# Layer one of a linear-attention and gMLP kernel: the last two token blocks of the transposed expansion as seven block products

## The chip, the cores and the metric

The kernel runs on one core of a Trainium2 chip. The metric is the device time of one execution in microseconds (us), the median of several runs. The engines have short names here, as in the profile: PE (TensorE, matrix products), PEld (its weight loads), DVE (VectorE), ACT (ScalarE), POOL (GpSimd) and SP (SyncE, which issues most DMAs). Each engine works through its own list of instructions in order and waits on semaphores for the others.

## The reference

Two layers, each of a linear attention (A) and a gated MLP with a mixing over tokens (B), on 2048 tokens of 512 features, all in fp32:

```python
def _A_ref(x, wqkv, wo):            # S=2048, D=512, 32 heads of 16
    q, k, v = split(x @ wqkv)
    phi = lambda t: where(t > 0, t + 1, exp(t)) + 1e-6
    pq, pk = phi(q), phi(k)
    kv, z = sum_s pk v, sum_s pk
    return ((pq kv) / (pq z + 1e-6)) @ wo

def _B_ref(x, w_in, w_sp, b_sp, w_out):      # w_in: 512 x 1792, w_sp: 2048 x 2048
    z = gelu(x @ w_in)                       # z1: first 896 columns, z2: last 896
    g = w_sp @ layernorm(z2) + b_sp
    return (z1 * g) @ w_out

x = x + A(ln(x));  x = x + B(ln(x));  x = x + A(ln(x));  x = x + B(ln(x))
```

## The kernel before

Every fp32 operand is split into a high and a low fp32r part (`high` on ACT, L132; `low` on DVE, L135), and a product is three matmuls (`mm3`, L146 to L148). The order on every engine is written out by hand: a scheduler does not move anything, so a line that is called earlier in Python stands earlier in the list of each engine that it uses. Tiles come from slot pools (22 `pages` of 128x512, 6 `quads`, 4 `bigs`, 8 PSUM `banks`), first freed, first used.

Per layer there are three stages.

* `P1`, the attention's first half. For each of 16 token blocks of 128 (step `s`): layer norm (`ln_a`, `ln_b`), transposition through a DMA (`Turn`), splitting (`T_high`, `T_low`), projections `K` and `Q` of 12 matmuls each with their `phi`, and a Gram product `Gmm`. In layer one this is `first`, which also splits the weights `wo` and `win2` (the list `side`) from step 5 on; in layer two it is `second`, which spreads those pieces one per step and interleaves units of `Inner` with them. `ln_b` stores the normalised block for the transposition; `x_high`/`x_low` split the Gram operand.
* `P2`, steps `s` = 1 to 18. For token block `s-1` the attention's end (`c`, `c2` adds the residual, `c_stats`, `c3` normalises and sends the block through a DMA transposition), for block `s-2` the splitting of the transposed block (`d_high` on ACT behind a DVE transposition at L327, `d_low`), for block `s-3` the token-major half of the expansion (`e`, 24 matmuls of 448 columns, then `e2` gelu on ACT, `e3` statistics, `e4` normalisation on ACT of the previous block with scales that POOL makes at L265 to L270). The transposed half, `z1`, is made per chunk `n` of 512 tokens and feature group `f` of 128: `f()` takes 12 matmuls, a gelu and a store.
* `P4`, the mixing over tokens by nested block products, and then a loop over 16 token blocks for the output product.

Layer two (`seven`) does not make `z1` of the chunks 2 and 3 by `f()`. It sees the two chunks, the feature groups (`g`, `g+3`) and the two halves of the contraction as a 2x2x2 block product and takes seven products (`P1` to `P7` in the class `P2`, `product` at L967 to L969, 6 matmuls each) for each of three `g`; the seventh feature group is made by `last_f`. This needs sums of the token blocks (`block_sums`, five DVE operations at L924 to L934 per block; `block_parts` splits them) and sums of blocks of `win1`. The latter are made once by the class `Make` during layer one's last token loop, split, stored to DRAM in `kept`, and read back by `fetch_sum` through POOL's DMA queue (L949). Five of the seven products are in `tail`, after the loop over `s`; the steps `P1(g)` and `P2(g)` are in `side`.

Two other side works matter. `Sums.tick` makes sums of `w_sp` for the mixing in layer one: at the steps in `TOKEN_TICKS` (5, 6, 8, 9, 11, 12, 14, 17) three POOL additions (L1178). `Inner` makes and stores split sums for a nested product; one unit is a DVE addition, an ACT `high` and a DVE `low`. In layer one `P2` makes eight units of `N2`:

```python
elif s == 12:
    own.begin(2)
elif s == 13 or 15 <= s:
    own.unit()
```

Of the kernel before, what the change touches and what calls it, by code (L numbers as in the profile page):

```python
# [15 lines left out]
P = 128  # L16
# [3 lines left out]
NT = S // P  # L20
NCHK = S // 512
NF = FH // P
# [62 lines left out]
def mixer_kernel(ctx: ExitStack, tc: tile.TileContext, x_in, wqkv, wo_d, win1_d, win2_d, wsp_d, bsp_d, wout_d,  # L85
                 ident_d, mask_d, out_d):
    nc = tc.nc
# [7 lines left out]
    pages = Slots(main, "pg", 22)  # L95
    quads = Slots(main, "qd", 6)
# [37 lines left out]
    def low(l, src, h):  # L134
        nc.vector.tensor_sub(l, src, h.bitcast(F32))  # L135
# [196 lines left out]
    class P1:  # L332
# [236 lines left out]

        def first(self, side):  # L570
            ND = NT - DEFER
            self.wv = quads.get([P, 4, 512])
            for s in range(1, NT + 2):
                self.loadx(s + 3)
                self.turn.load(s + 1)
                turned = 2 <= s < NT and s not in self.turn.by_pe
                if turned:
                    self.T_high(s)
                if s == 1:
                    if not self.kb:  # L580
                        self.K(0)
                    self.K(1)
                elif 2 < s <= NT:
                    self.K(s - 1)
                self.ln_a(s + 2)
                if turned:
                    self.T_low(s)
                if s <= NT:
                    self.K_phi(s - 1)
                if s <= ND:  # L590
                    self.Q(s - 1)
                if s == NT + 1:
                    self.late()
                if s <= NT:
                    self.xsplit(s - 1)
                    self.K_split(s - 1)
                if s + 1 < NT and s + 1 in self.turn.by_pe:
                    self.T(s + 1)
                self.ln_b(s + 2)
                if s <= ND:  # L600
                    self.Q_phi(s - 1)
                if s >= 2:
                    self.Gmm(s - 2)
                if s == NT + 1:
                    self.late_phi()
                if s <= 4:
                    c = s - 1
                    nc.sync.dma_start(self.wv[:, c, :], wqkv[c * P:(c + 1) * P, 1024:1536])
                else:
                    for _ in range(min(len(side), 1 if s < 6 else 2)):  # L610
                        side.popleft().piece()
                if s >= 4:
                    for w in list(side)[:1 if s < 5 else 2]:
                        w.fetch()

        def second(self, side):
            ND = NT - DEFER
# [126 lines left out]
    class P2:  # L744
        def __init__(self, p1):
            self.L = L = p1.L
            self.p1 = p1
            self.win1, self.win2 = w_in1(), p1.win2
            self.qturn, self.xturn = Turn(f"qt{L}", range(3), True), Turn(f"yt{L}", range(4))
            self.qp, self.qT, self.x, self.ms, self.xB, self.z, self.zms = {}, {}, {}, {}, {}, {}, {}  # L750
            self.fq = deque()
            self.fnext = []
            self.seven = self.L == 1
            self.held = deque()
            self.S, self.T, self.Tp, self.X = {}, {}, {}, {}

# [91 lines left out]
        def d_low(self, i):  # L848
            b, home, h, l = self.dpart
            low(l, b, h)  # L850
            n, k = divmod(i, 4)
            if self.seven and n == 3:
# [5 lines left out]
            if k == 3 and not (self.seven and n >= 2):  # L858
                self.fnext = [(n, f) for f in range(NF)]

        def e(self, i):
# [28 lines left out]
        def f(self):  # L890
            if not self.fq:
                return False
            n, f = self.fq.popleft()
            h, l = self.xT[n]
            w = self.win1
            b = banks.get(PAGE)
            for c in range(4):
                mm3(b, (w.h[:, f, c, :], w.l[:, f, c, :]), (h[:, c, :], l[:, c, :]), c == 0, c == 3)
            if f == NF - 1 and not (self.seven and n >= 2):
# [153 lines left out]

        def run(self, sums):
            w1 = self.win1
            own = inner["N1" if self.seven else "N2"]
            for s in range(1, NT + 3):
                self.loadx(s + 1)
                self.qturn.load(s + 1)
# [26 lines left out]
                else:  # L1086
# [19 lines left out]
                    if s <= NT + 1:  # L1106
                        if not sooner:
                            self.d_high(s - 2)
                        if not self.seven and 14 <= s < 18:
                            own.unit()  # L1110
                        self.d_low(s - 2)
                if s >= 15:
                    self.block_sums()
# [11 lines left out]
                    self.e3(s - 3)  # L1125
                self.f()
                self.f()
                if self.seven:
                    self.side(s)
                    if s == 5:  # L1130
                        own.begin(2)
                    elif 6 <= s:
                        own.staged()
                elif s == 12:
                    own.begin(2)
                elif s == 13 or 15 <= s:
                    own.unit()
# [4 lines left out]
                if not self.seven:  # L1142
                    sums.tick(s, TOKEN_TICKS)
                if s >= NT + 1 and not self.seven:
                    self.p4.fetch(s - NT - 1)
            self.e4(NT - 1)
            self.win2.free()

# [179 lines left out]
    class P4:  # L1328
# [394 lines left out]

        def run(self, nxt):
            p2 = self.p2
            if p2.seven:
                p2.tail(self)
            else:
# [4 lines left out]
                p2.win1.free()  # L1733
                self.prepare(1, 1)
                self.fetch(3)
                self.prepare(None, 2)
# [75 lines left out]
            make = Make()  # L1812
            for i in range(NT):
                self.loadx(i + 2)
                self.gates(2)
# [80 lines left out]
```

## Time and profile before

| | us |
|---|---|
| median of 3 runs | 1364.96 |
| lowest, highest | 1364.62, 1366.05 |
| the profiled execution's own time | 1364.2 |
| its span, first to last instruction | 1362.2 |
| PE busy | 1355.5 |
| DVE busy | 1007.3 |
| ACT busy | 628.5 |
| POOL busy | 465.9 |

The granted clock of PE is 1.000 over the whole span. A line of the timeline reads: start in us from the span's start, duration, engine, line of the kernel, operation, tiles, shapes, count, and in brackets the idle time before it with what ended it. A row of a window reads: the window, its length, then busy time and count for PE, PEld, DVE, ACT and POOL, the clock, the share of the DMA engines and GB/s. The matmuls are pipelined, so a PE that is busy is not yet one that starts matmuls as fast as it can; the count per window tells that.

Layer one's `P1` runs to about 125 us of the span, its `P2` from about 150 to 328 us, its `P4` to about 700 us; layer two's `P2` ends at 1005 us.

### The profile page before, as it was taken

What the parts mean: (1) busy time and instruction counts of PE and PEld (TensorE: products, weight loads), DVE (VectorE), ACT (ScalarE), POOL (GpSimd) and SP (SyncE); (2) the same over time, 40 slices, a digit from 0 to 9 for tenths busy, and PEclk for the clock granted to TensorE, in tenths of its full rate; (3) what the DMA queues carried; (4) which work ended last, traced back from release to release, by engine and by line L of the source; (5) the groups of instructions that cost most, each with busy time, mean ns of one, the idle gap of its engine ahead of it and who ended that gap; (6) DMA issues with size and microseconds to landing.
All of it is one profiled execution on the core that took longest, in us unless ns stands there. A gap on an engine that the chain in (4) does not pass through costs nothing.

```text
span 1362.2 us, 18282 instructions
## 1 busy us (share of the span) xinstructions
PE 1355.5 (100%) x6105; PEld 1135.3 (83%) x6105; DVE 1007.3 (74%) x1541; ACT 628.5 (46%) x1004; POOL 465.9 (34%) x539
## 2 busy tenths in 40 slices
PE   9999999999999999999999999999999999999998
PEld 7888888888888888888888888888888888888887
DVE  7775888765756789978778758877767798878642
ACT  6775543444433443443466655534465534533310
POOL 3333475433233137427421133533230011312240
PEclk9999999999999999999999999999999999999999
DMA  5541377877778988797976523666568798568552
GB/s 178 172 132 63 116 247 255 262 248 272 258 250 282 310 266 284 266 367 246 329 241 201 189 94 116 209 203 205 188 204 282 220 339 321 196 200 316 215 182 89
DMA packets 182622, 306.95 MB, mean 225 GB/s; under 512 B 15488, under 2 KB 67584, under 8 KB 178432
## 3 DMA queue, kind: packets, MB, share of 16 engines
q1 hardware_dynamic: 174320, 265.81, 59.2%
q0 software_dynamic: 6336, 36.70, 7.4%
q10 hardware_dynamic: 1872, 3.28, 0.7%
q8 instruction: 48, 0.79, 0.2%
q14 instruction: 46, 0.38, 0.1%
HBM read 208.47 MB, written 97.26 MB: 224 GB/s over the span
## 4 chain that ended last, share of the span: by engine, by line
PE 97%; DVE 2%; ACT 1%; issue 0%; POOL 0%; DVEq 0%; ACTq 0%; POOLq 0%
PE bank L148 19%; PE bank L146 19%; PE bank L147 19%; PE bank L1585 9%; PE bank L1584 9%; PE bank L1586 9%; PE bank L1517 4%; PE bank L1518 4%; PE bank L1515 4%; PE bank L969 1%; PE bank L968 1%; PE bank L967 1%; PE bank L708 1%; PE bank L288 0%; DVE pg L135 0%
## 5 line engine op out<-in xcount | busy, mean ns | idle before, releaser
L1584 PE MATMUL bank<-qd,pg 128*128 128x512 f32 x544 | 211.6, 389 | 0.0
L1585 PE MATMUL bank<-qd,pg 128*128 128x512 f32 x544 | 211.6, 389 | 0.0
L1586 PE MATMUL bank<-qd,pg 128*128 128x512 f32 x544 | 211.6, 389 | 0.0
L1431 DVE TENSOR_TENSOR qd<-qd,qd 128x1024 fp32r<-128x1024 f32 x104 | 143.9, 1383 | 69.9 <-ACT qd L1422 69.6
L1422 ACT ACTIVATE qd<-qd 128x1024 fp32r<-128x1024 f32 x104 | 110.0, 1058 | 125.6 <-DVE qd L1431 49.4
L132 ACT ACTIVATE pg<-pg 128x512 fp32r<-128x512 f32 (+1 forms) x154 | 94.8, 620 | 134.3 <-DVE pg L327 46.3
L148 PE MATMUL bank<-qd,pg 128*128 128x512 f32 x380 | 148.5, 391 | 0.2 <-DVE pg L135 0.2
L1178 POOL TENSOR_TENSOR pg<-pg,pg 128x512 f32<-128x512 f32 x64 | 95.6, 1493 | 136.4 <-DMA pg<-in_wsp_dram 88.2
L265 POOL TENSOR_SCALAR rs<-mv 128x1 f32<-128x1 f32 x95 | 46.7, 492 | 261.4 <-DVE mv L263 252.4
L276 ACT ACTIVATE pg<-pg,nb,rs 128x512 f32<-128x512 f32 x63 | 51.3, 814 | 171.3 <-POOL nb L270 159.7
L1606 POOL TENSOR_TENSOR bg<-bg,pg 128x512 f32<-128x512 f32 x56 | 90.9, 1634 | 112.4 <-DMA pg<-z 99.9
L135 DVE TENSOR_TENSOR pg<-pg,pg 128x512 fp32r<-128x512 f32 (+1 forms) x151 | 112.9, 748 | 14.7 <-ACT pg L132 6.4
L1584 PEld LDWEIGHTS bank<-qd,pg 128*128 128x128 f32 x544 | 102.1, 188 | 21.4
L1586 PEld LDWEIGHTS bank<-qd,pg 128*128 128x128 f32 x544 | 102.1, 188 | 21.1
L1585 PEld LDWEIGHTS bank<-qd,pg 128*128 128x128 f32 x544 | 102.1, 188 | 21.1
L146 PE MATMUL bank<-qd,pg 128*128 128x512 f32 x284 | 110.8, 390 | 0.0
L147 PE MATMUL bank<-qd,pg 128*128 128x512 f32 x284 | 110.6, 389 | 0.0
L327 DVE STREAM_TRANSPOSE pg<-pg 128x512 f32<-128x512 f32 x79 | 85.6, 1084 | 14.1 <-DMA z<-pg 4.6
L146 PE MATMUL bank<-bg,qd 128*128 128x448 f32 x256 | 94.0, 367 | 0.0
L147 PE MATMUL bank<-bg,qd 128*128 128x448 f32 x256 | 93.6, 366 | 0.0
L148 PE MATMUL bank<-bg,qd 128*128 128x448 f32 x256 | 93.4, 365 | 0.0
L1517 PE MATMUL bank<-qd,pg 128*128 128x512 f32 x224 | 87.3, 390 | 0.1
(214 smaller groups left out, 3163.3 us busy)
## 6 DMA issues: line engine op xcount, KB each, us to landing
qd<-s SPq DMA_DIRECT2D x64, 512.0 KB, 4.1
qd<-n POOLq DMA_DIRECT2D x32, 1024.0 KB, 8.5
pg<-in_wsp_dram SPq DMA_DIRECT2D x103, 256.0 KB, 4.5
qd<-in_wsp_dram SPq DMA_DIRECT2D x40, 512.0 KB, 4.4
n<-pg SPq DMA_DIRECT2D x70, 256.0 KB, 4.4
s<-pg SPq DMA_DIRECT2D x64, 256.0 KB, 4.1
pg<-z SPq DMA_DIRECT2D x56, 256.0 KB, 4.2
x<-pg SPq DMA_DIRECT2D x48, 256.0 KB, 3.0
```

The costliest lines, as they stand in the source:

```text
L132: nc.scalar.activation(h, src, AF.Copy)
L135: nc.vector.tensor_sub(l, src, h.bitcast(F32))
L146: nc.tensor.matmul(out, ah, bh, start=start, stop=False)
L147: nc.tensor.matmul(out, ah, bl, start=False, stop=False)
L148: nc.tensor.matmul(out, al, bh, start=False, stop=stop)
L1178: nc.gpsimd.tensor_tensor(t, a, b, op=OP.add)
L1422: nc.scalar.activation(wh, r, AF.Copy)
L1431: nc.vector.tensor_sub(wl, r, wh.bitcast(F32))
L1517: m(out[i], h[:, o, f], w[:, o, 1], start=False, stop=False, skip_group_check=True)
L1584: m(out, h[:, o], w[:, 0, j, :], start=start, stop=False, skip_group_check=True)
L1585: m(out, h[:, o], w[:, 1, j, :], start=False, stop=False, skip_group_check=True)
L1586: m(out, l[:, o], w[:, 0, j, :], start=False, stop=stop, skip_group_check=True)
```

## The change

1. In layer one, too, `z1` of the chunks 2 and 3 is made by seven products: the conditions on `seven` go, `side` and `tail` run in both layers. Instead of 14 groups of 12 matmuls there are 21 products of 6 and two groups of 12, 150 instead of 168. The twelve gelu results of these products are stored through ACT's DMA queue instead of SP's.
2. `Make` moves from layer one's last token loop to layer one's `P2`, each step at the end of an iteration `s`: fetches at 7, 10, 12, additions one step later, the two splits two and three steps later, stores behind them. For the third group that is: four additions at `s` = 13, a split each at 14 and 15.
3. The eight units of `N2` move from layer one's `P2` to `first`, steps 2 to 9, in the staged form of layer two, with two quads as their store.
4. `first` takes the order of `second`: `x_high` and `x_low` early, one piece of `side` per step from step 2, between `K_high` and `K_low`; `ln_b` goes behind `Q_phi`; `wv` is loaded at step 15.
5. `d_high` is called `sooner`, before `c3`, from step 14 on in layer one too. The first two fetches for `P4` move from the steps 17 and 18 into `tail`.

```diff
-MAKE_AT = 0, 2, 4
+MAKE_AT = 7, 10, 12
+ROW_UNITS = range(2, 10)
...
         def first(self, side):
             ND = NT - DEFER
-            self.wv = quads.get([P, 4, 512])
+            own = inner["N2"]
+            spare = quads.get([P, 2, 2, 512]), quads.get([P, 2, 2, 512])
+            own.home = Views(pages, *spare)
             for s in range(1, NT + 2):
                 self.loadx(s + 3)
                 self.turn.load(s + 1)
+                if s <= NT:
+                    self.x_high(s - 1)
...
-                self.ln_a(s + 2)
+                if s <= NT:
+                    self.x_low(s - 1)
                 if turned:
                     self.T_low(s)
+                self.ln_a(s + 2)
...
                 if s <= NT:
-                    self.xsplit(s - 1)
-                    self.K_split(s - 1)
+                    lows = deque()
+                    if s > 1 and side:
+                        for _ in range(min(len(side), 1 if s < 10 else 2)):
+                            side.popleft().piece(lows=lows)
+                    self.K_high(s - 1)
+                    own.staged(s in ROW_UNITS)
+                    for l, src, h, r in lows:
+                        low(l, src, h)
+                        pages.put(r)
+                    self.K_low(s - 1)
                 if s + 1 < NT and s + 1 in self.turn.by_pe:
                     self.T(s + 1)
-                self.ln_b(s + 2)
                 if s <= ND:
                     self.Q_phi(s - 1)
+                self.ln_b(s + 2)
...
     class P2:
         def run(self, sums):
             w1 = self.win1
-            own = inner["N1" if self.seven else "N2"]
+            own = inner["N1"]
+            make = Make() if self.L == 0 else None
...
-                    sooner = self.seven and s >= 14
+                    sooner = s >= 14
...
-                if self.seven:
-                    self.side(s)
-                    if s == 5:
-                        own.begin(2)
-                    elif 6 <= s:
-                        own.staged()
-                elif s == 12:
+                self.side(s)
+                if self.L == 0:
+                    make.step(s)
+                elif s == 5:
                     own.begin(2)
-                elif s == 13 or 15 <= s:
-                    own.unit()
+                elif 6 <= s:
+                    own.staged()
...
     class P4:
         def run(self, nxt):
             p2 = self.p2
-            if p2.seven:
-                p2.tail(self)
-            else:
-                self.prepare(0, 0)
-                self.fetch(2)
-                while p2.f():
-                    pass
-                ...
+            p2.tail(self)
...
-                    make.step(i)
                     self.join(i, nxt)
```

`Make.step`, which is not changed, is what is called at the new place:

```python
def split(self, g):
    r = self.raw[g].pop()
    h = pages.get(PAGE, F32R)
    split(h, r.bitcast(F32R), r)      # high on ACT, then low on DVE
    self.part[g] = h.bitcast(F32), r, h
```

More of the change, by code (lines that the diff above doesn't have):

```diff
@@ L605, in first @@
                     self.late_phi()
-                if s <= 4:
-                    c = s - 1
-                    nc.sync.dma_start(self.wv[:, c, :], wqkv[c * P:(c + 1) * P, 1024:1536])
-                else:
[L610 to L614, printed above, removed]
+                for w in list(side)[:1 if s < 9 else 2]:
+                    w.fetch()
+                if s == 1:
+                    own.begin(2, 1)
+                if s == NT - 1:
+                    own.home.close()
+                    own.home = pages
+                    quads.put(*spare)
+                    self.wv = quads.get([P, 4, 512])
+                    for c in range(4):
+                        nc.sync.dma_start(self.wv[:, c, :], wqkv[c * P:(c + 1) * P, 1024:1536])
         def second(self, side):
@@ L851, in d_low @@
             n, k = divmod(i, 4)
-            if self.seven and n == 3:
+            if n == 3:
                 self.held.append((k, b))
@@ L857, in d_low @@
                 pages.put(self.xB.pop(i))
-            if k == 3 and not (self.seven and n >= 2):
+            if k == 3 and n < 2:
                 self.fnext = [(n, f) for f in range(NF)]
@@ L898, in f @@
                 mm3(b, (w.h[:, f, c, :], w.l[:, f, c, :]), (h[:, c, :], l[:, c, :]), c == 0, c == 3)
-            if f == NF - 1 and not (self.seven and n >= 2):
+            if f == NF - 1 and n < 2:
                 quads.put(*self.xT.pop(n))
@@ L1108, in run @@
                             self.d_high(s - 2)
-                        if not self.seven and 14 <= s < 18:
-                            own.unit()
                         self.d_low(s - 2)
@@ L1127, in run @@
                 self.f()
-                if self.seven:
-                    self.side(s)
-                    if s == 5:
-                        own.begin(2)
-                    elif 6 <= s:
-                        own.staged()
-                elif s == 12:
+                self.side(s)
+                if self.L == 0:
+                    make.step(s)
+                elif s == 5:
                     own.begin(2)
-                elif s == 13 or 15 <= s:
-                    own.unit()
+                elif 6 <= s:
+                    own.staged()
                 self.fq.extend(self.fnext)
@@ L1141, in run @@
                 w1.fetch()
-                if not self.seven:
+                if self.L == 0:
                     sums.tick(s, TOKEN_TICKS)
-                if s >= NT + 1 and not self.seven:
-                    self.p4.fetch(s - NT - 1)
             self.e4(NT - 1)
@@ L1811, in run @@
             pages.put(*self.bs)
-            make = Make()
             for i in range(NT):
```

6 lines of the change are left out of this document (removed).

## The prediction

> **What bounds the kernel now.** I read the page first, then PE's windows, then the timeline around the places that the change touches, in layer one and in layer two, which already does what is now added.
>
> ```profile
> PE 1355.5 (100%) x6105; PEld 1135.3 (83%) x6105; DVE 1007.3 (74%) x1541; ACT 628.5 (46%) x1004; POOL 465.9 (34%) x539
> PE 97%; DVE 2%; ACT 1%; issue 0%; POOL 0%; DVEq 0%; ACTq 0%; POOLq 0%
> 0.00:100.00 100.00, 97.41 (x425) 79.35 (x426) 73.98 (x126) 68.72 (x115) 34.76 (x59) 1.00 0.51 161
> 500.00:600.00 100.00, 100.00 (x443) 82.84 (x442) 87.87 (x100) 38.76 (x63) 51.68 (x36) 1.00 0.86 294
> 700.00:800.00 100.00, 100.00 (x441) 82.30 (x440) 77.89 (x113) 65.33 (x114) 18.33 (x14) 1.00 0.59 193
> ```
>
> PE is the bound, and almost without a hole: 97% of the chain that ended last is PE, and in the full windows it starts 443 matmuls in 100 us, one each 0.226 us, at full clock. Two things follow. A matmul that goes is worth 0.226 us, wherever it goes. And any new wait of PE is paid in full, since no hole is there to take it up. So the question is only whether DVE, ACT and POOL still deliver before PE arrives.
>
> **What goes.** 168 matmuls become 150: 18 x 0.226 = 4.1 us. That is the whole gain. `Make` leaves a token loop in which PE started 441 matmuls in 100 us, so nothing comes free there; the eight `N2` units leave steps of `P2` in which they delayed no matmul.
>
> **What shrinks with it.** The f() groups were also PE's padding. From the start of `c` for block 13 (the head of step 14) to the start of `e` for block 14 (the head of step 17), layer one now runs layer two's PE list, so I read PE's pace and the length of each link there:
>
> ```profile
> 959.38 0.39 PE L146 MATMUL bank<-qd,pg 128*128 128x512 f32 x1
> 981.50 1.15 DVE L261 BATCH_NORM_STATS2 st<-z_z 128x6 f32<-128x448 f32 x2
> 982.88 0.63 DVE L987 TENSOR_TENSOR pg<-pg,bank 128x512 f32<-128x512 f32 x1
> 983.55 0.63 ACT L910 ACTIVATE pg<-pg 128x512 f32<-128x512 f32 x1 [2.29 <-DVE pg L987]
> 984.65 0.60 ACT L975 ACTIVATE pg<-bank 128x512 f32<-128x512 f32 x1 [0.47 <-ACT pg L910]
> 983.43 0.68 DVE L135 TENSOR_TENSOR pg<-pg,pg 128x512 fp32r<-128x512 f32 x1
> 984.03 0.68 DVE L819 TENSOR_TENSOR pg<-pg,bank 128x512 f32<-128x512 f32 x1
> 985.64 1.06 DVE L327 STREAM_TRANSPOSE pg<-pg 128x512 f32<-128x512 f32 x1
> 986.74 0.63 ACT L132 ACTIVATE qd<-pg 128x512 fp32r<-128x512 f32 x1 [1.48 <-DVE pg L327]
> 989.02 0.36 PE L146 MATMUL bank<-bg,qd 128*128 128x448 f32 x1
> ```
>
> PE needs block 14's high part 989.02 - 959.38 = 29.64 us after `c(13)`; layer two has it at 986.74 + 0.63, that is at 27.99, with 1.65 us to spare.
>
> **Place A, block 14.** Layer one differs in one link. At the end of step 15 `Make` splits: its ACT `high` stands behind the gelu (L910) and the copy (L975) of that step, and its DVE `low` waits for that `high`; behind the `low`, on DVE, stand `c2` of block 15 (L819), its statistics and the transposition of block 14 (L327), and for that PE waits. Layer two's L135 at 983.43 is a `low` whose `high` was made a step earlier and waits for nothing. Layer one also comes later to this point, as its own timeline shows:
>
> ```profile
> 277.08 0.39 PE L146 MATMUL bank<-qd,pg 128*128 128x512 f32 x1
> 293.75 1.50 DVE L135 TENSOR_TENSOR pg<-pg,pg 128x512 fp32r<-128x512 f32 x1 [0.70 <-ACT pg L132]
> 293.41 4.36 POOL L1178 TENSOR_TENSOR pg<-pg,pg 128x512 f32<-128x512 f32 x3
> 299.78 0.81 ACT L276 ACTIVATE pg<-pg,nb,rs 128x512 f32<-128x512 f32 x1 [6.07 <-POOL nb L270]
> 300.50 0.61 ACT L132 ACTIVATE qd<-pg 128x512 fp32r<-128x512 f32 x1
> 303.13 1.15 DVE L261 BATCH_NORM_STATS2 st<-z_z 128x6 f32<-128x448 f32 x2 [1.28 <-ACT z_z L877]
> ```
>
> Three POOL additions of tick 14 take 4.36 us ahead of the scale for block 14 (299.78 waits for POOL's nb); the statistics of block 12 start at 303.13 - 277.08 = 26.05. `sooner` takes the 0.61 us of the ACT copy at 300.50 out of the way: 25.4. This start does not hang on the f() groups that go, since the link before it is POOL, not PE. On from there by layer two's links: to the `P2` addition 1.38 (26.8), to the gelu 0.67 (27.5), to the copy 1.10 (28.6), copy 0.60 (29.2), `Make`'s high 0.6 (29.8), its low 0.65 with the hand-over (30.4), from `c2` to the transposition 1.61 (32.0), to ACT 1.10 (33.1), high 0.63 (33.8). PE is there at 29.6: a wait of **4.1 us**. The ends: if the statistics started at layer two's 981.50 - 959.38 = 22.1 it would be 0.8; another 1 us if `Make`'s four additions at step 13 push the whole line back (each some 0.42 us, by the row of L213 below), 5.1. I take 4.1, since 25.4 is layer one's own row.
>
> ```profile
> L213 DVE TENSOR_TENSOR pg<-pg,pg 128x256 f32<-128x256 f32 x3 | 1.3, 425 | 0.1
> ```
>
> **Place B, the end of step 18 and the tail.** Layer two again:
>
> ```profile
> 997.99 0.36 PE L146 MATMUL bank<-bg,qd 128*128 128x448 f32 x1
> 1003.33 0.69 DVE L924 TENSOR_TENSOR pg<-qd,qd 128x512 f32<-128x512 f32 x1
> 1006.90 3.65 DVE L135 TENSOR_TENSOR qd<-pg,qd 128x512 fp32r<-128x512 f32 x6
> 1001.97 2.14 POOL L949 DMA_DIRECT2D pg<-win_sums  x4
> 1007.09 0.54 POOL L265 TENSOR_SCALAR rs<-mv 128x1 f32<-128x1 f32 x1 [2.98 <-DVE mv L263]
> 1010.04 1.14 ACT L276 ACTIVATE z_z<-z_z,nb,rs 128x896 f32<-128x896 f32 x1 [1.83 <-POOL nb L270]
> 1009.69 0.39 PE L967 MATMUL bank<-qd,pg 128*128 128x512 f32 x1
> 1012.17 1.29 DVE L1009 TENSOR_TENSOR pg<-pg,bank 128x512 f32<-128x512 f32 x2 [1.62 <-ACT pg L975]
> 1013.77 0.39 PE L967 MATMUL bank<-qd,pg 128*128 128x512 f32 x1
> 995.04 0.69 DVE L135 TENSOR_TENSOR qd<-pg,qd 128x512 fp32r<-128x512 f32 x1 [0.70 <-ACT qd L132]
> ```
>
> `P6` (1009.69) needs the first of six `low`s (1006.90 + 0.6: 2.2 us to spare); `P7` (1013.77) needs the first addition at L1009 (done about 1012.86: 0.9 to spare), which waits for a copy on ACT behind block 15's normalisation (1010.04), which waits for POOL. In layer one tick 17 puts three more POOL additions into the 2.98 us in which POOL waited before 1007.09: 4.36 from 1004.11 ends at 1008.5, **1.4 us** late. Second, DVE and ACT reach this step later: block 15's low is ready at 995.73 in layer two, 10.1 us after the transposition of block 14, and PE wants it 2.26 later; in layer one PE leaves the wait of A 1.73 us after that transposition (1.10 + 0.63) and wants block 15 after another 8.97 (997.99 - 989.02), so only 0.6 is left, **1.65 us** less. Together 1.4 + 1.65 - 0.9 = 2.15 us of wait. Third, the additions run beside the sums and the `low`s, as at 293.41, where a DVE `low` took 1.50 us beside an addition against 0.68 elsewhere. If all three block DVE so, 3 x 0.82 = 2.5 more, 4.7. I take 3.4, the middle, since part of the six `low`s is behind the additions.
>
> [...]
>
> **Place C, the start.** `ln_b` of block 3 (ACT at 18.76) goes behind `Q_phi`'s two ACT operations (19.46, 20.08: 1.3 us), and SP, in order, holds the first loads of `wo` and `N2` behind its store:
>
> ```profile
> 18.76 0.80 ACT L276 ACTIVATE pg<-pg,nb,rs 128x512 f32<-128x512 f32 x1
> 19.46 0.59 ACT L414 ACTIVATE z_q<-bank 128x512 f32<-128x512 f32 x1
> 20.08 0.63 ACT L415 ACTIVATE z_q<-z_q 128x512 f32<-128x512 f32 x1
> 19.59 0.38 SPq L312 DMA_DIRECT2D xt<-pg  x1
> 20.01 0.50 SPq L608 DMA_DIRECT2D qd<-in_wqkv_dram  x1
> pg<-in_wsp_dram SPq DMA_DIRECT2D x103, 256.0 KB, 4.5
> 28.13 0.69 DVE L135 TENSOR_TENSOR pg<-pg,pg 128x512 fp32r<-128x512 f32 x1
> ```
>
> The store goes to 20.9, the third load behind it to about 22.4, landing 26.9; the unit's addition and two `low`s (0.69 each at most) end near 28.9, where the Gram product of block 1 wants them near 28. Between 0 (the load lands as fast as others) and 1.5 (ACT waits for `wo` too); I take 0.5. Later steps cost nothing: eight units add 16 DVE operations of 0.69, 11 us, to 74 busy in the first 100, and the cover is DVE's idle quarter. Without it each unit would cost up to 1.4.
>
> **The sum.** -4.1 + 4.1 + 3.4 + 0.5 = +3.9 us on the profiled execution's 1364.2 (span 1362.2 and 2.0 around it): 1368.1. The median of the runs shown is 0.8 above that execution: **1368.9**.
>
> **The rivals.**
> *Layer one goes as layer two does*: no wait, 1364.96 - 4.1 = 1360.9. For it: the same steps in layer two leave 1.65, 2.2 and 0.9 us to spare. Against it: those steps have no tick, and no `low` that waits in the same step. It decides at step 15: if `c2` of block 15 starts by 26.3 us after `c(13)`, there is no wait at A, and B stays under 1. Chance 0.15.
> *Half*: A is 1.5 and B 2.15, because DVE catches up before step 15 in its idle time; -4.1 + 1.5 + 2.15 + 0.5 = 0: 1365.0. For it: DVE and ACT have idle time in 290 to 305. Chance 0.20.
> *The full lock*: each POOL addition of the ticks 14 and 17 excludes DVE; A 5.1, B 4.7: +6.2, 1371.2. For it the 1.50 row, against it that DVE's PSUM additions and statistics ran on undisturbed there. [...] Chance 0.15.
> That the change does not take the matmuls away can't be: they are counted in the instruction list.
>
> **How the numbers follow.** The forecast has 0.50; its own range is 1366.5 to 1371, about 0.05 of it below 1367.7. A measurement of this kernel can tell about 0.2%, 2.7 us, from no change: faster is under 1362.2, slower over 1367.7. Faster: the first rival, 0.15. Same: 0.20 + 0.05 = 0.25. Slower: 0.45 + 0.15 = 0.60. The range leaves out the first rival and 0.05 at the top: 1363.0 to 1372.5.
>
> **What would show it.** In the profile after: 18 matmuls fewer; PE idle before the first `e` matmul of block 14 in layer one, released by ACT's L132, some 4 us; a DVE `low` of `Make` at step 15 that waits for ACT and ends after 30 us from `c(13)`; PE idle at `P6` or `P7` of layer one's tail, released by DVE; a small one near 28 us. No PE idle at step 17 would make the forecast wrong at A, none in the tail at B; a wait in `P4`'s first steps would be one that I did not price.

## The result: 24 us slower, and most of it at places that the prediction had left out

| | before | after |
|---|---|---|
| median, us | 1364.79 | 1389.03 |
| lowest to highest, us | 1364.29 to 1366.05 | 1388.42 to 1390.66 |
| span of the profiled execution, us | 1362.2 | 1387.1 |

The ratio is 1.0178 (95% interval 1.0160 to 1.0196). The changed kernel's lines stand a little lower: `high` and `low` are L133 and L136 there, a load by SP L129, the transposition L328, `c2` L835, the five block sums L940 to L950, `product` L983 to L985, the copy L991, the tail's addition L1025, `Make`'s store L228, a tick's store L1183 and its POOL additions L1188, POOL's running sum of K L440.

The page of the changed kernel, busy time and the chain that ended last:

```profile
PE 1365.0 (98%) x6087; PEld 1132.7 (82%) x6087; DVE 1032.3 (74%) x1581; ACT 638.2 (46%) x1021; POOL 470.4 (34%) x551
PE 75%; DVE 8%; DMA 6%; ACT 5%; issue 2%; POOL 2%; SPq 1%; ACTq 0%; DVEq 0%; POOLq 0%
```

The 18 matmuls are gone (6087 against 6105). But PE is only 75% of the chain, where it was 97%, and DMA, absent before, holds 6%. DVE still has a quarter of its time idle: no engine beside PE has become full.

Where PE lost time is read from the matmuls that it ran in the same stretches. Windows of before:

```profile
20.00:85.00 65.00, 65.00 (x288) 53.85 (x287) 48.00 (x78) 45.99 (x79) 23.23 (x35) 1.00 0.54 171
85.00:125.00 40.00, 40.00 (x179) 33.11 (x178) 25.57 (x40) 23.82 (x40) 13.59 (x16) 1.00 0.29 87
255.00:320.00 65.00, 65.00 (x302) 56.46 (x302) 44.04 (x69) 27.35 (x46) 26.31 (x39) 1.00 0.80 270
320.00:345.00 25.00, 25.00 (x115) 21.27 (x114) 9.06 (x18) 10.95 (x17) 7.03 (x9) 1.00 0.76 243
345.00:370.00 25.00, 25.00 (x112) 20.68 (x111) 19.47 (x28) 11.02 (x14) 5.53 (x4) 1.00 0.70 245
```

The same windows of after:

```profile
20.00:85.00 65.00, 64.61 (x284) 52.79 (x283) 52.53 (x86) 46.57 (x81) 21.35 (x32) 1.00 0.65 202
85.00:125.00 40.00, 38.02 (x154) 27.58 (x153) 29.77 (x46) 25.63 (x43) 13.10 (x19) 1.00 0.55 173
255.00:320.00 65.00, 59.19 (x253) 47.63 (x252) 44.17 (x76) 22.81 (x37) 27.01 (x38) 0.97 0.73 241
320.00:345.00 25.00, 21.20 (x93) 18.10 (x92) 16.71 (x32) 12.79 (x22) 8.39 (x20) 0.93 0.70 225
345.00:370.00 25.00, 22.44 (x98) 17.88 (x97) 15.56 (x27) 13.84 (x24) 9.60 (x11) 1.00 0.74 235
```

A matmul less is the window's length over its count before, 0.22 us. So 0.9 us went between 20 and 85 us (288 - 284 = 4 matmuls), **5.6 in the rest of the first stage** (25), **10.5 between 255 and 320** (49), 4.8 at block 14 (22) and 3.1 in the tail (14). Another 0.9 us is at 382 (130 matmuls against 134 from 370 to 400) and 0.8 in the first 20 us (69 against 72). Together 26.6, less 4.1 for the matmuls that went: 22.5 of the 24.9 us between the spans. The count is rough, since matmuls of 448 columns are shorter than those of 512 and the two kernels do not have the same mix in a window. Taken start by start from the trace, against the median spacing (0.203 us behind a matmul of 448 columns, 0.227 behind one of 512), after loses 28.9 us more than before, 10.6 from 255 to 320 us and 5.8 at block 14 among them; less 4.1 that is 24.8. The prediction had priced the windows of block 14 and the tail, and nearly rightly in size. It had put the two bold ones at nothing.

### The profile page after: what moved, and what is told of

It reads as the page before. It is cut to its first block, busy times and chain, and to the rows that moved or that the text cites. A ratio compares the mean times of both kernels' runs of the same rounds, so it can differ in the third digit from the quotient of the medians.

```text
span 1387.1 us, 18361 instructions
## 1 busy us (share of the span) xinstructions
PE 1365.0 (98%) x6087; PEld 1132.7 (82%) x6087; DVE 1032.3 (74%) x1581; ACT 638.2 (46%) x1021; POOL 470.4 (34%) x551
## 4 chain that ended last, share of the span: by engine, by line
PE 75%; DVE 8%; DMA 6%; ACT 5%; issue 2%; POOL 2%; SPq 1%; ACTq 0%; DVEq 0%; POOLq 0%
PE bank L149 11%; PE bank L147 11%; PE bank L148 11%; PE bank L1595 9%; PE bank L1596 9%; PE bank L1594 9%; PE bank L1527 3%; PE bank L1528 3%; PE bank L1525 3%; DVE st L262 1%; DVE pg L136 1%; DVE pg L328 1%; PE bank L983 1%; PE bank L985 1%; PE bank L984 1%
## 5 line engine op out<-in xcount | busy, mean ns | idle before, releaser
L1595 PE MATMUL bank<-qd,pg 128*128 128x512 f32 x544 | 211.7, 389 | 0.8 <-DVE qd L1441 0.8
L1596 PE MATMUL bank<-qd,pg 128*128 128x512 f32 x544 | 211.6, 389 | 0.0
L1594 PE MATMUL bank<-qd,pg 128*128 128x512 f32 x544 | 211.6, 389 | 0.0
L133 ACT ACTIVATE pg<-pg 128x512 fp32r<-128x512 f32 (+1 forms) x146 | 90.2, 622 | 142.7 <-DVE pg L328 41.9
L149 PE MATMUL bank<-qd,pg 128*128 128x512 f32 x380 | 149.6, 394 | 0.8 <-DVE pg L136 0.8
L1188 POOL TENSOR_TENSOR pg<-pg,pg 128x512 f32<-128x512 f32 x64 | 94.6, 1478 | 137.4 <-DMA pg<-in_wsp_dram 118.1
L266 POOL TENSOR_SCALAR rs<-mv 128x1 f32<-128x1 f32 x95 | 42.1, 444 | 286.6 <-DVE mv L264 274.9
L136 DVE TENSOR_TENSOR pg<-pg,pg 128x512 fp32r<-128x512 f32 (+1 forms) x143 | 106.5, 745 | 22.7 <-ACT pg L133 13.6
L1595 PEld LDWEIGHTS bank<-qd,pg 128*128 128x128 f32 x544 | 102.1, 188 | 22.6 <-DVE qd L1441 1.2
L1594 PEld LDWEIGHTS bank<-qd,pg 128*128 128x128 f32 x544 | 102.1, 188 | 21.4
L1596 PEld LDWEIGHTS bank<-qd,pg 128*128 128x128 f32 x544 | 102.1, 188 | 20.9
L147 PE MATMUL bank<-qd,pg 128*128 128x512 f32 x284 | 111.1, 391 | 0.6 <-ACT pg L133 0.6
L148 PE MATMUL bank<-qd,pg 128*128 128x512 f32 x284 | 110.6, 390 | 0.0
L147 PE MATMUL bank<-bg,qd 128*128 128x448 f32 x256 | 95.6, 374 | 8.5 <-ACT qd L133 8.5
L328 DVE STREAM_TRANSPOSE pg<-pg 128x512 f32<-128x512 f32 x79 | 85.9, 1087 | 17.5 <-DMA z<-pg 6.1
L149 PE MATMUL bank<-bg,qd 128*128 128x448 f32 x256 | 95.4, 373 | 0.2
L148 PE MATMUL bank<-bg,qd 128*128 128x448 f32 x256 | 94.8, 370 | 0.0
L149 PEld LDWEIGHTS bank<-qd,pg 128*128 128x128 f32 x380 | 71.3, 188 | 21.0 <-DVE pg L136 6.4
```

What stands on the lines that cost most here:

```text
L147: nc.tensor.matmul(out, ah, bh, start=start, stop=False)
L148: nc.tensor.matmul(out, ah, bl, start=False, stop=False)
L149: nc.tensor.matmul(out, al, bh, start=False, stop=stop)
L328: nc.vector.transpose(y.rearrange("p c (t m) -> p m c t", m=4), r.rearrange("p (m c j) -> p m c j", m=4, c=4))
L1188: nc.gpsimd.tensor_tensor(t, a, b, op=OP.add)
L1594: m(out, h[:, o], w[:, 0, j, :], start=start, stop=False, skip_group_check=True)
```

## The experiments

What PE waited for in after (us in total, times, longest), in stretches around 264, 295, 329 and 350 to 390 us:

```profile
PE bank L147 <- ACT qd L133: 2.0, 1, 2.0
...
PE bank L147 <- ACT qd L133: 2.7, 2, 2.0
...
PE bank L147 <- ACT qd L133: 3.8, 1, 3.8
...
PE bank L984 <- DVE qd L136: 1.4, 1, 1.4
PE bank L983 <- DVE pg L1025: 1.2, 1, 1.2
PE bank L1595 <- DVE qd L1441: 0.8, 1, 0.8
```

The timeline of after ahead of the first of them:

```profile
253.95 1.16 SPq L228 DMA_DIRECT2D win_sums<-pg  x2
255.16 1.47 SPq L129 DMA_DIRECT2D pg<-in_win_dram  x2
256.68 1.52 SPq L1183 DMA_DIRECT2D s<-pg  x3
256.93 1.08 DVE L328 STREAM_TRANSPOSE pg<-pg 128x512 f32<-128x512 f32 x1 [2.69 <-DMA win_sums<-pg]
261.28 0.69 DVE L136 TENSOR_TENSOR pg<-pg,pg 128x512 fp32r<-128x512 f32 x1 [2.17 <-DMA s<-pg]
261.89 0.68 DVE L835 TENSOR_TENSOR pg<-pg,bank 128x512 f32<-128x512 f32 x1
265.95 0.62 ACT L133 ACTIVATE qd<-pg 128x512 fp32r<-128x512 f32 x1
266.62 0.47 PE L147 MATMUL bank<-bg,qd 128*128 128x448 f32 x1 [2.03 <-ACT qd L133]
```

DVE waits twice, not for data but for a place to write: its output pages were given back by stores of the step before, and those have not landed (`win_sums<-pg` is a store of `Make`, `s<-pg` one of a tick). Behind these waits stand the residual addition, the statistics and the next block's `high`, for which PE waits. The pool hands its 22 pages out in the order in which they were freed. Followed through the program, the twelve pages that the attention's split takes in the steps 11 to 14 (the waits shown are in step 11) were all given back behind stores of `f()`, `Make` or a tick, issued at the end of the step before; in before that holds for three of the twelve, and the others came free earlier in that step.

In the first stage DVE and ACT wait for places too (after, 17 to 130 us; `n<-qd` is the store of an N2 unit, L440 an addition on POOL that reads a page):

```profile
DVE pg L328 <- POOL pg L440: 4.2, 3, 1.4
...
ACT qd L133 <- DMA n<-qd: 3.8, 2, 1.9
```

### The first stage

**first_only**: before with the new `first`, N2 in it and not in `P2`.

> The kernel before, with the new order of layer one's first stage and the eight N2 units in it, nothing else. PE's waits of the changed kernel by place: 0.9 us up to 8 us of the span, 0.4 near 29, 5.7 between 92 and 118, 10.0 between 260 and 320 (slowed matmuls included), 5.5 at block 14, 3.1 in the tail, 1.1 at 382, against 4.1 for the matmuls that go. Theory (the places add up, and the first three belong to the first stage alone): 1364.8 + 7.3 = 1372. Rival (the delay of the first stage is a part of the waits behind it, or is made up in them, since all engines come late together): the span is within 2 us of the kernel before, 1365 to 1367.

1372.28 against 1364.93 us, ratio 1.0053 (1.0038 to 1.0068): +7.35. The parts add up; nothing of it is made up or hidden later.

**order_only**: the same without the units there (they stay in `P2`).

```diff
-                    own.staged(s in ROW_UNITS)
```

> The kernel before, with the new order of the first stage but the N2 units left where they were, in layer one's second stage. Theory N2 (the units' loads and stores on SP, and ACT standing in front of late weight loads, use up the slack, and what is left at step 10 is too little): the waits between 92 and 118 us go, +0.5 us at the start at most: 1365.5. Rival ORDER (x_high takes two pages ahead of the transposition, which then gets the page that POOL's sum of the step before has just given back; a loop of POOL, DVE, ACT, longer than PE's 6.8 us a step): the 5.7 us stay, 1371.

1367.31, +2.4: between the two theories. The new order alone costs a third.

**n2_old_order**: the units in `first`, its old order. Two things differ besides the order: a unit stands at the end of a step instead of between `K_high` and `K_low`, and `wv` is still loaded at step 15, since the units take its quad.

```diff
                 if s == NT + 1:
                     self.late_phi()
+                if s <= NT:
+                    own.staged(s in ROW_UNITS)
```

> The kernel before, with the eight N2 units in the first stage (one staged unit at the end of each of the steps 2 to 9), but the first stage's old order. Together with the two runs of the first stage it makes a square: new order without N2 cost 2.4 us, new order with N2 7.3. Theory ORDER (the units only hurt because the new order leaves the transposition no older page, and one weight load a step right behind them): under 2 us, 1365 to 1367. Rival LOAD (the units' ACT, DVE and SP work costs its 5 us in either order): 1370.

1376.87 against 1365.02, +11.9: both theories wrong. In the old order, and at the end of the steps, the units cost even more. ACT and SP wait for places (17 to 130 us):

```profile
ACT qd L133 <- DMA n<-qd: 6.1, 2, 3.3
...
SPq L1233 <- DMA n<-qd: 8.4, 3, 3.5
```

ACT stands in a unit's `high`, and SP in front of a unit's load, until an earlier store has given back one of eight places in two quads. SP's queue holds the stores of the normalised blocks, the loads of the transposed ones and the units' stores in one order, in which SP waits 58.3 us, in 13 waits, for ACT's normalised blocks and 9.2, in 8, for their stores, so the place comes back late. In first_only the same two rows read 2.8 us in 2 waits and 8.7 in 3: ACT waits more here, SP does not. So places are a part of the 11.9 us, and where the rest comes from is not shown.

**zacc_later**: after, with the page of the old running sum of K held one step longer.

```diff
-                pages.put(self.zacc)
+                if self.zold is not None:
+                    pages.put(self.zold)
+                self.zold = self.zacc
```

> The changed kernel; in layer one's first stage the page of the old running sum of K is given back one step later. In the changed kernel, from step 11 on, the transposition of the next block (DVE) gets the page that POOL's addition to this sum, at the end of the step before, has just read, and waits for it (4.2 us in 3 waits of DVE, and a loop DVE 1.1, ACT 0.64, DVE 0.69 and so on, POOL 1.3 of 6.7 us a step, where PE has work for 5.4). Theory PAGE ORDER: that loop is the stall between 92 and 118 us; with another page there it falls from 5.3 us of PE's time to under 1.5, total 1389 - 4 = 1385. Rival BUSY (DVE and ACT are simply too full there after the N2 units): unchanged, 1389.

1388.60, no faster in all. In its place it did half of what was expected: the window of zacc_later from 85 to 125 us shows 164 matmuls (154 in after: 2.2 us), and DVE no longer waits for L440. But 5 matmuls more were lost from 20 to 85 us (279), and 7 more from 255 to 345.

```profile
85.00:125.00 40.00, 38.46 (x164) 29.93 (x163) 31.34 (x48) 28.66 (x49) 14.32 (x19) 1.00 0.65 201
```

**first_slower** and **first_repaired**: first_only with the units spread out; then also the page later and one weight piece a step to the end. The last two were not tried one at a time.

```diff
-ROW_UNITS = range(2, 10)
+ROW_UNITS = 3, 4, 5, 7, 8, 9, 11, 12
...
-min(len(side), 1 if s < 10 else 2)
+min(len(side), 1)
```

> The kernel before with the new first stage and N2 in it (7.3 us slower than before), but the eight units at the steps 3, 4, 5, 7, 8, 9, 11, 12 instead of 2 to 9. Theory SLOTS (ACT stands in a unit's split for a slot that a store, queued on SP behind a load that itself waits, has not yet given back: 2.8 us in 2 waits of ACT; and the first unit waits for its first load near 28 us): the wait near 28 us and 2 us of the rest go, 1364.9 + 4 = 1369. Rival LOAD (DVE's and ACT's work for the units): 1372, or more since two units now meet two weight pieces a step.

> The same, and the running sum's page given back a step later, and one weight piece a step to the end (steps 2 to 12) instead of two from step 10. Theory: with slots, page order and double pieces gone, the first stage costs under 1.5 us: 1366. Rival (something else in it, as the units' bare load): 1369 or more.

1368.68 and 1366.86 against 1365.27: +3.4 and +1.6 (ratio 1.0011, 1.0002 to 1.0021). As the theory had it: with the same eight units at a slower pace the stage costs half, and ACT's waits for `n<-qd` are gone; with the page order and the double pieces gone all but 1.6 us is back. The window of first_repaired:

```profile
85.00:125.00 40.00, 40.00 (x178) 33.11 (x178) 30.05 (x46) 25.27 (x44) 13.26 (x17) 1.00 0.61 195
```

DVE is as busy there as in after (30.05 against 29.77 us): its idle time was indeed enough. What was not is when places came free, and the pace of the units and pieces.

### The second stage and the tail

**first_make**: first_only, and `Make` moved as in after; `z1` still by `f()`.

> The one before with the new first stage and N2 there, and Make moved into layer one's second stage as well (steps 7 to 16), but z1 still by f() groups. Theory (Make alone brings the waits between 260 and 320 us): PE waits there for some 7 to 10 us, total 1372 + 8 = 1380. Rival (it is the seven products that bring them: no f() groups to pad PE): PE waits under 1 us there, 1372 to 1373.

1381.91, 9.6 above first_only. `Make` alone does it, f() groups or not:

```profile
255.00:320.00 65.00, 58.83 (x255) 48.17 (x254) 41.75 (x70) 21.38 (x36) 25.81 (x39) 0.97 0.77 254
```

**make_on_act**: after, with `Make`'s eighteen transfers (six loads and twelve stores; the expectation counts twelve) issued by ACT (`nc.scalar.dma_start` for `nc.sync.dma_start`).

> The changed kernel with Make's loads and stores issued by ACT instead of SP. In the changed kernel SP issues a burst of 15 transfers from 252.5 to 261.6 us, Make's four among them, and DVE waits for pages that these stores give back (2.7 us for win_sums, 2.2 for s). Theory QUEUE (what is late is a page or a load behind that burst): PE's waits at 264 and 293 us go down from 2.2 us each to under 1, 1389 - 3 to -6 = 1383 to 1386. Rival ENGINES (Make's additions and splits on DVE and ACT are what is late): nothing changes or it grows by ACT's 12 more issues of 0.34 us, 1389 to 1391.

1392.29: the queue theory was wrong. Without `Make`'s share of SP's burst PE lost no less: ACT waited 12.3 us, in two waits, for stores of ticks that give pages back. The edit also puts `Make`'s loads into ACT's own order, so it does not show what SP's burst alone is worth.

**make_in_z**: after, with nine of `Make`'s twelve buffers in tiles `z` that lie idle at that time.

```diff
-            self.raw[g] = [load(win1_d[g + 3]), load(win1_d[g])]
+            self.raw[g] = [self.tile(i, f"w{g}") for i in (MAKE_AT[g] + 2, MAKE_AT[g] + 1)]
```

> The changed kernel with nine of Make's twelve buffers in tiles z that lie idle at that time (a block's tile between the end of q and its gelu) instead of pages; the same instructions and transfers in the same order on every engine. Theory PAGES (with Make's buffers in the pool, the attention's split gets pages that stores of Make and of the ticks have just given back, and waits for those stores to land): PE's waits between 260 and 320 us fall from 10.0 to under 2.5 us, total 1389 - 8 = 1381; block 14 (5.5) and the tail (3.1) stay within 1 us. Rival ENGINES (Make's additions and splits on DVE and ACT): unchanged, 1388 to 1390.

1384.67, 4.4 us less: the theory of pages, with half of its size. Same instructions, same queues, other places. From 255 to 320 us PE runs 275 matmuls instead of 253 (302 in before), 4.7 of the 10.5 us; and none of the twelve pages of the steps 11 to 14 comes from a store of `f()`, `Make` or a tick any more. Of PE's waits from 255 to 345 us (6.1 with a small one) 3.8 is block 14's, which did not change; 2.3 are left of the 5.6 before it (2.0 and 2.7 above and 0.9 in two small rows), and none at 264.

```profile
PE bank L148 <- ACT qd L134: 5.9, 3, 3.8
```

**ticks_later**: after, with the ticks of 12, 14 and 17 moved into the mixing.

```diff
-TOKEN_TICKS = (5, 6, 8, 9, 11, 12, 14, 17)
-MIX_TICKS = (1, 4, 7, 8, 10, 12, 14, 16, ...
+TOKEN_TICKS = (5, 6, 8, 9, 11)
+MIX_TICKS = (1, 2, 4, 5, 7, 8, 10, 11, 12, 14, 16, ...
```

> The changed kernel with the ticks of the steps 12, 14 and 17 moved into the mixing (at 2, 5 and 11 there). Theory PAGES: the pages that the ticks hold and the stores that give them back go from the steps 12 to 14, so the waits between 260 and 320 us fall from 10.0 to about 3 us. Theory of the prediction, places A and B: three POOL additions (4.4 us) no longer stand ahead of the scale for block 14, nor ahead of block 15's in the tail: block 14 falls from 5.5 us to some 2 (what is left is Make's split), the tail from 3.1 to 1.5. Together 1389 - 7 - 3.5 - 1.6 = 1377, if the mixing hides three more ticks; rival (the ticks do nothing to either): 1388 to 1390.

1388.36. Where the ticks were, it went part of the way as forecast: block 14's wait fell from 3.8 to 2.5 us, the tail's from 2.6 to 0.4, and from 255 to 320 us 19 matmuls came back of 49. Where they went, it cost the same again. PE's waits from 320 to 470 us (the profile is of the slowest of four executions, 1392.44 us; the fastest took 1386.21):

```profile
PE bank L1594 <- DVE bg L1632: 3.4, 1, 3.4
PE bank L1594 <- DVE bg L1641: 2.8, 1, 2.8
PE bank L147 <- ACT qd L133: 2.5, 1, 2.5
PE bank L1595 <- DVE qd L1441: 0.7, 1, 0.7
PE bank L983 <- DVE pg L1025: 0.4, 1, 0.4
```

**combined**, all three edits (zacc_later, make_in_z, ticks_later):

> The three edits together: the sum's page later, nine of Make's buffers in idle z tiles, three ticks in the mixing. Theory: the effects add up where they touch different places, 1389 - 4 (92 to 118 us) - 9 (260 to 320) - 3.5 (block 14) - 1.6 (tail) = 1371, still slower than before by what is left at the start (1.3), block 14, the tail and the mixing's first steps. Rival (one place's waits hide another's: with one gone the next is longer): 1376 or more.

1379.93: closer to the rival. The mixing runs 27 matmuls less from 400 to 480 us than before (328 against 355, 6.1 us), and from 255 to 320 us 30 are still missing (272 against 302); the largest wait there is block 14's, 2.5 us. The waits before it, 5.6 us in after, are down to 0.8.

**make_sooner**: combined, with `MAKE_AT = 6, 9, 11`.

> The kernel with the three edits together, and Make one step earlier (6, 9, 11 instead of 7, 10, 12), so that its last split falls on step 14 and none on step 15, where block 15's addition, statistics and block 14's transposition stand behind it on DVE. With the ticks gone from there, PE still waited 2.7 us for block 14. Theory (the prediction's link at A: this wait is Make's split of step 15): the wait falls under 0.8 us, 1380 - 2.3 = 1377.6. Rival (the wait comes from DVE's and ACT's lateness before): 2 us or more stay, 1379 to 1380.

1375.39, 4.5 less, and from 255 to 345 us the view of PE's waits has no row any more. Its windows there:

```profile
255.00:320.00 65.00, 64.93 (x299) 55.43 (x298) 49.76 (x86) 30.93 (x51) 22.68 (x44) 1.00 0.67 216
320.00:345.00 25.00, 25.00 (x114) 20.89 (x113) 17.19 (x34) 15.73 (x28) 8.70 (x15) 1.00 0.72 217
```

So the wait for block 14 that the ticks had left was `Make`'s, and its split in step 15 is the link that the expectation named; the edit moves the fetches and additions a step, too. DVE is busier there than in after (49.8 against 44.2 us), and PE waits for nothing.

### All together

**repaired** (first stage as in n2_old_order, make_in_z, `Make` one step earlier, two ticks moved to the mixing's steps 6 and 9):

> The changed kernel with what the runs point to: the first stage's old order with N2 at the end of the steps, nine of Make's buffers in idle z tiles, Make one step earlier, and the ticks of 14 and 17 moved into the mixing at steps in which four pages are free (6 and 9). Theory (the causes found are the whole of it): PE's waits fall to the start's 1.5, some 1.5 between 260 and 310, 0.5 at block 14, 1 at the mixing's first steps: 1364.8 - 4.1 + 4.5 = 1365, even with before. Rival (a cause is missing, or the moved ticks cost the mixing 3 us each as before): 1369 to 1374.

1378.44: neither; the first stage's old order cost most of what it cost in n2_old_order (from 20 to 125 us 422 matmuls, there 412, in before 467).

**all_repaired** (first_repaired's first stage, make_in_z, `Make` one step earlier, three ticks moved to step 3 and the mixing's 6 and 9), **final_a** (`Make`'s transfers on ACT, the tick of step 3 at 7) and **final_b** (that tick at the mixing's step 2):

> The changed kernel with all of it: this first stage, nine of Make's buffers in idle z tiles, Make one step earlier, and the ticks of 12, 14 and 17 moved to step 3 and to the mixing's steps 6 and 9. Theory (the causes found are the whole loss): 1364.9 - 4.1 for the matmuls + 1.5 first stage + 1 second stage + 1 at the mixing's first steps = 1364.3, even with before or a little under it. Rival (one of them only moved): 1368 to 1372.

> The kernel with all repairs, with Make's loads and stores issued by ACT, and the tick of step 3 at step 7 instead. Theory QUEUE: with Make's twelve transfers off SP, the loads of x and qt come in time; the waits at 234 and 286 us (1.6 and 0.8 us of PE's time) go, and that at 172 (1.9) with the tick: 1369.1 - 4 = 1365, even with before. Rival: a tick at step 7 costs what it cost at step 3, and ACT's issues are paid: 1368 to 1370.

> The same with that tick at the mixing's step 2 instead of step 7. Theory QUEUE: the second stage has under 1 us of waits, the mixing as before 1.1: 1364.9 - 4.1 + 0.6 + 1 + 1.1 = 1363.5, at best 0.1% faster than before. Rival (a tick among the mixing's first steps, whose pages the gelu stores give back late, holds SP as it did in the run with three moved ticks): 3 us more, 1366 to 1367.

1369.13 (ratio 1.0027, 1.0018 to 1.0036), 1369.11 and 1372.83; final_b's executions spread from 1368.64 to 1374.94, and its profile is of the fastest. So the repairs bring back 20 of the 28 us that the change lost beside its gain of 4.1, and no version beats before. Two of the moved ticks cost nothing at the mixing's steps 6 and 9: all_repaired runs 354 matmuls from 400 to 480 us, as after does. The third makes PE wait wherever it was put: near 172 and 234 us in all_repaired (tick at 3), at 232 in final_a (at 7), at 435 in final_b (in the mixing), and the former places are then clear. How a tick at step 3 or 7 leads to a wait near 233 us is not shown, and whether there is an order in which the 4.1 us are kept stays open.

## Why the prediction was wrong, point by point

**Place A** was right. Forecast 4.1 us; measured a wait of 3.8, released as told. The timeline of after:

```profile
289.90 0.50 PE L147 MATMUL bank<-qd,pg 128*128 128x512 f32 x1 [0.41 <-ACT pg L133]
...
320.67 1.15 DVE L262 BATCH_NORM_STATS2 st<-z_z 128x6 f32<-128x448 f32 x2 [0.80 <-ACT z_z L893]
323.78 0.60 ACT L991 ACTIVATE pg<-bank 128x512 f32<-128x512 f32 x1 [0.42 <-ACT pg L926]
324.27 0.62 ACT L133 ACTIVATE pg<-pg 128x512 fp32r<-128x512 f32 x1
324.93 0.69 DVE L136 TENSOR_TENSOR pg<-pg,pg 128x512 fp32r<-128x512 f32 x1 [2.24 <-ACT pg L133]
325.54 0.68 DVE L835 TENSOR_TENSOR pg<-pg,bank 128x512 f32<-128x512 f32 x1
327.18 1.08 DVE L328 STREAM_TRANSPOSE pg<-pg 128x512 f32<-128x512 f32 x1
328.29 0.63 ACT L133 ACTIVATE qd<-pg 128x512 fp32r<-128x512 f32 x1 [3.40 <-DVE pg L328]
328.97 0.47 PE L147 MATMUL bank<-bg,qd 128*128 128x448 f32 x1 [3.80 <-ACT qd L133]
```

Copy, `Make`'s high, its low after 2.24 us of idle DVE, `c2`, transposition, high, PE: link by link. From the statistics to the end of the high it is 8.25 us (forecast 8.4). Counted from `c(13)` (289.90) both sides are some 5.5 us later than forecast, since PE itself had waited in between: the statistics start at 30.8 (25.4) and PE arrives at 35.3 (29.6), so that the difference came out is in part luck. The shares were off: ticks 1.3 (ticks_later), `Make` the other 2.5 (make_sooner); the prediction had given the ticks most.

**Place B**: forecast 3.4, measured 1.4 + 1.2 = 2.6, and the ticks carry 2.2 of it (ticks_later). That the size came near is partly luck, for the way was another. The tail in after's timeline (the first row is an earlier block's sum):

```profile
318.31 0.42 DVE L947 TENSOR_TENSOR pg<-pg,pg 128x256 f32<-128x256 f32 x1
...
345.88 4.48 POOL L1188 TENSOR_TENSOR pg<-pg,pg 128x512 f32<-128x512 f32 x3
346.98 0.81 DVE L940 TENSOR_TENSOR pg<-qd,qd 128x512 f32<-128x512 f32 x1 [1.89 <-DMA z<-pg]
347.82 1.40 DVE L947 TENSOR_TENSOR pg<-pg,pg 128x256 f32<-128x256 f32 x1
349.25 1.40 DVE L948 TENSOR_TENSOR pg<-pg,pg 128x256 f32<-128x256 f32 x1
352.79 0.54 POOL L266 TENSOR_SCALAR rs<-mv 128x1 f32<-128x1 f32 x1 [2.43 <-DVE mv L264]
```

The prediction's first term was POOL, busy with tick 17 when block 15's scale is due, 1.4 us late. But POOL is done with the tick at 350.36 and then waits 2.43 us for DVE's statistics: DVE is late. It had waited 1.89 us for a place that a gelu's store gives back, of which the prediction has nothing, and it lost 2.0 us in two sums, the prediction's third term. In ticks_later neither is there, and PE's wait in the tail is 0.4 us. Such a sum takes 0.42 us alone and 1.40 beside additions of 1.49, and each of the two ends 0.3 to 0.4 us behind the end of an addition (the three taken as equally long); that it waits until the running one is done is the author's reading of these ends. The six `low`s start at 352.61, behind the additions, and take 3.65 us, as the six in layer two of before do.

**Place C**: 0.5 forecast, 0.4 waited near 29 us in after, a gap of 0.8 us between two matmul starts. That it fits is luck: in the five other kernels with the same first stage (first_only, first_make, make_on_act, make_in_z, ticks_later) PE waits 1.3 to 1.6 us there, a gap of 1.7 to 2.0.

**The step that failed** is "Later steps cost nothing: eight units add 16 DVE operations ... and the cover is DVE's idle quarter", and beside it that `Make` was priced only by its additions and its split in step 15. Both counted engine time, and that count holds: first_repaired and make_sooner give DVE at least as much to do as after in these windows (30.1 against 29.8 us, 49.8 against 44.2), and PE runs 178 of 179 and 299 of 302 matmuls. What was put at nothing without a reason is storage. From 255 to 320 us 10.5 us went because steps waited for places that stores gave back too late: with other places alone 4.7 came back (make_in_z), and with the ticks gone and `Make` a step earlier, too, nearly all (make_sooner). That this remainder is storage as well is argued, not shown, since those edits also move engine work. In the first stage 2.2 of the 5.6 us came back in their window when a page that POOL still read was handed out later (zacc_later, which lost 1.1 more before it); the rest came back with the units' slower pace and the single weight pieces, and how it is shared between places and pace is not shown. The prediction never asked which page each moved step takes, who freed it and when that store lands; before's own waits held the hint, DVE and ACT waiting for `s<-pg` and `z<-pg` in the second stage (from 150 to 330 us ACT 5.9 us in one wait for `s<-pg`, DVE 3.3 in two for `z<-pg`). In after, PE waits four times for ACT's `z_h` between 85 and 120 us, 0.4 us each; in zacc_later, with the one page held longer, one wait of 0.6 is left, which fits a place that comes back late.

Two smaller terms were missing: 0.9 us at the mixing's first steps, which the prediction named as unpriced, and the slow matmuls after a long wait (below), 1.2 us at block 14 alone (from 329.4 to 332.7 us of after 10 matmuls at clock 0.50, where 16 fit at their later spacing of 0.207 us). Its rivals all shared the gap: each varied A and B, none let another stage stall.

## What to carry to other kernels

When a step is moved in a schedule with a fixed pool of buffers, follow each buffer it takes to who frees the one that is handed out next: a place that an engine reads last is free when that read is done, one that a store reads last when the store lands, here 3.0 to 4.4 us after SP issues it (medians of `z<-pg` and `s<-pg` in after). Price a moved step by engine time, by queue and by storage, and look in the trace of before for waits on stores ("DMA x<-pg") as the sign that the pool is already short. Engines that are idle a quarter of the time do not show that.

## What the hardware did that was not expected

After a long wait PE ran at half its clock for some 3 us. Windows of after around the wait at 264 us (the number behind POOL's is the granted clock):

```profile
262.00:266.60 4.60, 2.59 (x11) 1.80 (x10) 3.01 (x6) 1.37 (x3) 2.56 (x4) 1.00 0.94 333
268.20:271.20 3.00, 3.00 (x10) 2.66 (x9) 2.82 (x7) 1.22 (x3) 1.36 (x3) 0.50 0.52 160
271.20:275.00 3.80, 3.80 (x19) 3.33 (x18) 2.75 (x5) 0.64 (x1) 3.64 (x4) 0.99 1.02 329
```

Ten matmuls run in the 3.0 us at clock 0.50, 19 in the 3.8 behind. A wait of 2.0 us (2.4 between two starts) thus cost some 1.6 more. It does not follow each time: a second gap of 2.4 us in the same trace, before 295.5 us, has clock 1.00 behind it. In after the mean clock of the next 4 us is 1.00 behind gaps of 1.55 and 1.79 us, 0.66 and 1.00 behind the two of 2.4, and 0.57 behind that of 4.2 at block 14. Behind the first 15 us of thirteen of these kernels, none of the 15 gaps from 1.3 to 1.9 us between two matmul starts lowered the clock of the next 4 us, and 19 of the 29 above 2.1 us did (to 0.50 to 0.73 in the mean of these 4 us). So an idle PE of 2.0 us was enough here, while gaps of 3.4 and 3.8 us in two kernels had no slow stretch behind them: it depends on more than the gap's length, and on what is not shown.
